# A spatial gating product in Strassen's form, with the second phase of the kernel in written order

## The chip, the cores and the metric

The kernel runs on one core of a Trainium2 chip. The metric is the device time of one execution in microseconds. Three executions of the kernel before took 1106.92, 685.29 and 686.55 us, median 686.55 us; the profiled execution took 685.1 us.

## What is computed

Three stages for a batch of 4, a sequence S of 768 and a model width of 384. First gated linear attention (8 heads of 48), then a low-rank mix along the sequence and an MLP, then a gated MLP with a product along the sequence. All results are wanted in float32; the changed part is in the last stage:

```python
h = gelu(x @ w_in)                       # 768 x 1024 for each batch
u, v = h[..., :512], h[..., 512:]
v_n = (v - mean(v)) / sqrt(var(v) + 1e-6) * g_ln
v_s = einsum('ts,bsd->btd', w_sg, v_n) + b_sg[None, :, None]   # 768 x 768 times 768 x 512
out = x + (u * v_s) @ w_out
```

## The kernel before

Phase 1 computes attention and the first MLP, batch by batch; `mlp(b, hf, fill)` runs the 12 steps of one half (384 rows of the sequence) of a batch, and in each step `fill(i)` issues a piece of other work: for batches 0 to 2 the attention of the next batch, for batch 3 (`fill_last`, 24 steps for the two halves) the loading of phase 2's weights. TensorE takes every operand as a sum of two numbers, a high part `h` that ScalarE copies out in the matmul's own format and a low part `l`, the rest, that POOL subtracts (`split`, L145 to L147); a product is then three matmuls, hh, hl and lh (`products`). In `fill_last` each of the first 12 steps narrows and splits a piece of w_in and w_out, each of the other 12 splits one twelfth of w_sg into the buffer that held a piece of the first MLP's weights, and the last step splits batch 0 (`make_hl`, its tiles are `uh` and `ul`).

Phase 2 has four kinds of blocks, each a run of matmuls into one PSUM bank:

- `v_block` (6 for each batch, 9 matmuls of 512 columns): one chunk of 128 rows of the v half; then gelu (ScalarE Square L114, VectorE L115, ScalarE Tanh L116, VectorE L117), the mean and variance (VectorE L123, L124), 1/sqrt on POOL (L125, L126), the normalising VectorE operation L127, and a split into `vnh` and `vnl`.
- `u_block` (8, 9 matmuls of 384 columns): the u half, transposed, with gelu.
- `g_block` (8, 18 matmuls of 384 columns): the product with w_sg for 128 channels and half of the sequence; VectorE scales and adds the bias (L832) and multiplies by u (L833); a split into `gth` and `gtl`.
- `o_block` (6, 12 matmuls of 384 columns): the product with w_out, the residual and the store to HBM.

The blocks go in the order v(b), o(b-1), u(b), g(b). A block takes the next of the 8 PSUM banks, so block n waits until the operations that read block n-8 are done. Phase 1 stands under `manual_schedule`: its instructions run as the program writes them on each engine. This is closed (`fixed.close()`) after the last MLP, and phase 2's order on each engine comes from the framework's scheduler. All DMAs are issued by SP, in order.

Of the kernel before, what the change touches and what calls it, by code (L numbers as in the profile page):

```python
# [30 lines left out]
HT = S // 2  # L31
PR = 112
# [5 lines left out]
UNIT = 384  # L38
# [14 lines left out]
def kernel(  # L53
# [79 lines left out]
    def fast(st):  # L133
# [41 lines left out]
        fixed = st.enter_context(ExitStack())  # L175
        fixed.enter_context(tc.manual_schedule())
# [557 lines left out]

        todo = [(flat(win[0]), flat(win[1]), w_in, i) for i in range(0, KD * FF2, UNIT)]
# [4 lines left out]
        wsg = [[flat(x) for x in w1s[f]] for f in range(KF1)]  # L740
        here = {}

        def fetch_last(i):
            if i < KF1:
                _, _, src, at = todo[i]
                here[i] = fetch(stage, [(ALL, src[:, at:at + UNIT])], 128, UNIT)
            elif i < 2 * KF1:
                here[i] = stage.tile([128, UNIT], F32, tag="z", name="z")
                nc.sync.dma_start(here[i], w_sg[:, (i - KF1) * HT:(i - KF1 + 1) * HT])
# [7 lines left out]
        def fill_last(i):  # L757
# [3 lines left out]
            if i < KF1:  # L761
                here[i] = narrow_last(narrow_first(stage, here[i], 128, UNIT))[0]
            else:
                split(*wsg[i - KF1], here.pop(i))
            fetch_last(i + 2)
# [4 lines left out]
            elif i == 2 * KF1 - 1:  # L770
                make_hl(work2, 0, 0)
                make_hl(work2, 0, 1)
# [6 lines left out]
        fixed.close()  # L779
# [4 lines left out]
        vp = p2.enter_context(sp("vp", 1))  # L784
        tm = p2.enter_context(sp("tm", 2))
        stage_cm.__exit__(None, None, None)
        gp = p2.enter_context(sp("gp", 2, "right"))
# [4 lines left out]
        turn = [0]  # L792
# [6 lines left out]
        vn, ug, gt = {}, {}, {}  # L799

        def v_block(b, s):
            if s == 0:
                vn[b] = [vp.tile([128, NCH, HF], F32R, tag="vn" + x, name="vn" + x) for x in "hl"]
            if s % 3 == 0 and (b, s // 3) not in hl:
                make_hl(work2, b, s // 3)
# [4 lines left out]
            x = tm.tile([128, HF], F32, tag="t1", name="t1", bufs=4)  # L810
            gelu2(p, tm.tile([128, HF], F32, tag="t0", name="t0", bufs=3), x, x)
            normalise(tm, eps, x, x)
            split(vn[b][0][:, s, :], vn[b][1][:, s, :], x)

        def u_block(b, hf, m):
# [5 lines left out]
            x = ug[b][:, m, hf * HT:(hf + 1) * HT]  # L821
            gelu2(p, tm.tile([128, HF], F32, tag="t0", name="t0", bufs=3)[:, :HT], x, x)

        def g_block(b, hf, m):
            if m == 0:
                gt[b, hf] = [gp.tile([128, KH, HT], F32R, tag="gt" + x, name="gt" + x) for x in "hl"]
            p = any_bank([128, HT])
            t = slice(hf * HT, (hf + 1) * HT)
            mm(p, [x for s in range(NCH) for x in products(cut(vn[b], ALL, s, slice(m * 128, m * 128 + 128)),
                                                           wsg[s * 2 + hf])])  # L830
            x = tm.tile([128, HF], F32, tag="t0", name="t0", bufs=3)[:, :HT]
            vec.scalar_tensor_tensor(x, p, gcol[:, m:m + 1], bsg[:, t], op0=ALU.mult, op1=ALU.add)  # L832
            vec.tensor_tensor(x, x, ug[b][:, m, t], op=ALU.mult)  # L833
            split(gt[b, hf][0][:, m, :], gt[b, hf][1][:, m, :], x)

        def o_block(b, hf, d):
# [3 lines left out]
            mm(p, x + [x for m in range(KH) for x in products(cut(wout, ALL, m, slice(d * 128, d * 128 + 128)),  # L840
                                                              cut(gt[b, hf], ALL, m))])
            o = xT[b][:, d, hf * HT:(hf + 1) * HT]
            if last:
                act.activation(o, p, ACTF.Copy, scale=0.5)
            else:
                vec.scalar_tensor_tensor(o, p, 0.5, o, op0=ALU.mult, op1=ALU.add)
            nc.sync.dma_start(out[b, d * 128:(d + 1) * 128, hf * HT:(hf + 1) * HT], o)

        act.activation(two, ident, ACTF.Copy, scale=2.0)
        for b in range(B + 1):  # L850
            if b < B:
                for s in range(NCH):
                    v_block(b, s)
            if b:
                for hf in range(2):
                    for d in range(KD):
                        o_block(b - 1, hf, d)
            if b < B:
                for hf in range(2):
                    for m in range(KH):  # L860
                        u_block(b, hf, m)
                for hf in range(2):
                    for m in range(KH):
                        g_block(b, hf, m)
        p2.close()

    def general(b, st):
# [100 lines left out]
        for s in range(NCH):  # L968
# [5 lines left out]
            normalise(wk, eps, t1, vn[:, s, :])  # L974
# [86 lines left out]
```

## Time and profile before

| | |
|---|---|
| profiled execution | 685.1 us |
| its span | 683.0 us |
| TensorE busy | 673.2 us (99%) |
| VectorE, ScalarE, POOL busy | 409.6, 265.6, 260.5 us |
| chain of waits that ended last | 88% TensorE, 6% DMA |

The time of an execution is its span and some 2 us around it. Phase 1 ends, and phase 2 begins, at 428.20 us in the span. In the timelines a matmul's row is longer than its distance to the next, since matmuls overlap; the pace of TensorE is read from the starts. DMA traffic is at 394 and 396 GB/s in the page's second and third slices of 40, where phase 1 loads its weights, and at 60 GB/s or less in most slices of phase 2.

### The profile page before, as it was taken

How to read it: one execution, taken by the hardware profiler on the slowest of the kernel's cores; microseconds unless marked ns; L12 is line 12 of the kernel's file. 1: busy time of each engine (PE TensorE's matmuls, PEld its weight loads, DVE VectorE, ACT ScalarE, POOL GpSimd, SP SyncE). 2: the span in 40 equal slices, each digit the busy share in tenths (PEclk: the TensorE clock that was granted, in tenths of full speed). 3: DMA queues.
4: the chain of work that ended last, by engine and by line, in shares of the span. 5: the costliest groups of instructions: out<-in, count | busy, mean ns of one | idle time of the engine just before them, and what ended most of it. 6: DMA issues, size and time to landing. Idle time of an engine off the chain costs nothing.

```text
span 683.0 us, 12753 instructions
## 1 busy us (share of the span) xinstructions
PE 673.2 (99%) x5153; PEld 640.8 (94%) x5153; DVE 409.6 (60%) x719; ACT 265.6 (39%) x547; POOL 260.5 (38%) x324
## 2 busy tenths in 40 slices
PE   7999999999999999999999999999999999999997
PEld 5889899999999999999999999899899999989997
DVE  7988776444655444655458821694675486458532
ACT  4787333222323222323234423572543246143410
POOL 5789922112311212311124533674444254335030
PEclk9999999999999999999999999999999999999999
DMA  8990113301111211110024321000010001001002
GB/s 319 394 396 27 59 61 98 99 38 59 59 60 59 75 43 59 60 59 1 2 70 139 93 72 46 24 2 1 1 69 1 1 12 59 1 1 70 1 1 74
DMA packets 22098, 47.10 MB, mean 69 GB/s; under 512 B 2576, under 2 KB 10640, under 8 KB 22032
## 3 DMA queue, kind: packets, MB, share of 16 engines
q1 hardware_dynamic: 22032, 46.21, 19.7%
q8 instruction: 42, 0.69, 0.4%
q14 instruction: 24, 0.20, 0.1%
HBM read 41.49 MB, written 4.72 MB: 68 GB/s over the span
## 4 chain that ended last, share of the span: by engine, by line
PE 88%; DMA 6%; POOL 3%; DVE 1%; issue 1%; ACT 1%; SPq 0%; DVEq 0%; ACTq 0%; POOLq 0%
PE ps_h L81 29%; PE ps_ch L555 20%; PE ps_at L81 14%; PE ps_ch L81 14%; PE ps_at L396 3%; PE ps_at L428 3%; DMA raw<-in_w_dram 2%; DMA fqk<-in_fqk_dram 2%; POOL w L303 2%; PE ps_at L433 1%; PE ps_at L410 1%; DMA xT<-in_fqk_dram 1%; PE ps_at L504 1%; PE ps_at L480 1%; PE ps_at L450 1%; DVE ps_at L272 1%
## 5 line engine op out<-in xcount | busy, mean ns | idle before, releaser
L575 DVE SCALAR_TENSOR_TENSOR al<-ps_h,ah 128x384 fp32r<-128x384 f32 x96 | 53.4, 556 | 121.6 <-ACT ah L574 121.1
L81 PE MATMUL ps_h<-uh,w 128*128 128x384 f32 x576 | 120.2, 343 | 0.0
L555 PE MATMUL ps_ch<-ah,w 128*128 128x384 f32 x576 | 115.3, 334 | 0.0
L555 PEld LDWEIGHTS ps_ch<-ah,w 128*128 128x128 f32 x576 | 101.2, 188 | 0.0
L81 PEld LDWEIGHTS ps_h<-uh,w 128*128 128x128 f32 x576 | 98.8, 188 | 1.9
L574 ACT ACTIVATE ah<-ps_h 128x384 fp32r<-128x384 f32 x96 | 47.1, 491 | 122.6 <-PE ps_h L81 122.5
L555 PE MATMUL ps_ch<-al,w 128*128 128x384 f32 x288 | 65.6, 335 | 0.0
L81 PE MATMUL ps_h<-ul,w 128*128 128x384 f32 x288 | 65.4, 334 | 0.0
L147 POOL TENSOR_TENSOR ul<-xT,uh 128x384 fp32r<-128x384 f32 x45 | 47.6, 1086 | 46.7 <-ACT uh L146 45.8
L147 POOL TENSOR_TENSOR gtl<-t,gth 128x384 fp32r<-128x384 f32 x32 | 32.8, 1027 | 73.5 <-ACT gth L146 73.5
L81 PEld LDWEIGHTS ps_h<-ul,w 128*128 128x128 f32 x288 | 51.5, 188 | 0.1
L555 PEld LDWEIGHTS ps_ch<-al,w 128*128 128x128 f32 x288 | 51.3, 188 | 0.0
L146 ACT ACTIVATE gth<-t 128x384 fp32r<-128x384 f32 x32 | 16.8, 525 | 78.0 <-DVE t L833 78.0
L363 POOL TENSOR_TENSOR fall<-g,fqk 112x4 f32<-112x4 f32 x15 | 3.1, 208 | 110.2 <-DVE g L358 110.2
L147 POOL TENSOR_TENSOR xl<-x,xh 128x384 fp32r<-128x384 f32 x18 | 18.2, 1013 | 53.1 <-ACT xh L146 51.8
L402 DVE TENSOR_TENSOR am<-ps_at,mask 128x512 f32<-128x512 f32 x43 | 27.9, 685 | 17.2 <-PE ps_at L396 17.0
L147 POOL TENSOR_TENSOR vnl<-t,vnh 128x512 fp32r<-128x512 f32 x24 | 31.1, 1296 | 17.8 <-ACT vnh L146 17.8
L81 PE MATMUL ps_ch<-w,vnh 128*128 128x384 f32 x144 | 36.7, 335 | 0.1
L81 PE MATMUL ps_at<-w,vnh 128*128 128x384 f32 x144 | 36.6, 334 | 0.0
L367 POOL TENSOR_TENSOR fqk<-fqk,g 112x512 f32<-112x512 f32 x21 | 26.9, 1283 | 23.9 <-issue 21.2
L396 PEld LDWEIGHTS ps_at<-fqk 48*128 48x128 f32 x336 | 21.5, 187 | 9.6 <-issue 4.3
L396 PE MATMUL ps_at<-fqk 48*128 48x128 f32 x336 | 25.8, 285 | 3.6 <-POOL fqk L381 2.2
(234 smaller groups left out, 1494.3 us busy)
## 6 DMA issues: line engine op xcount, KB each, us to landing
fqk<-in_fqk_dram SPq DMA_DIRECT2D x36, 384.0 KB, 3.7
raw<-in_w_dram SPq DMA_DIRECT2D x24, 384.0 KB, 7.9
out_dram<-xT SPq DMA_DIRECT2D x24, 192.0 KB, 2.0
v<-in_v_dram SPq DMA_DIRECT2D x21, 192.0 KB, 3.9
raw<-in_w_in_dram SPq DMA_DIRECT2D x8, 384.0 KB, 3.2
xT<-in_fqk_dram SPq DMA_DIRECT2D x6, 384.0 KB, 5.8
z<-in_w_sg_dram SPq DMA_DIRECT2D x12, 192.0 KB, 2.4
fqk<-in_fqk_dram SPq DMA_DIRECT2D x8, 256.0 KB, 4.9
```

What stands on the lines that cost most here:

```text
L81: pe.matmul(ps, lhsT=l, rhs=r, start=(i == 0), stop=(i == n - 1))
L146: act.activation(hi, src, ACTF.Copy)
L147: eng.tensor_tensor(lo, src, hi.bitcast(F32), op=ALU.subtract)
L272: vec.scalar_tensor_tensor(zi, zi, 3, low, op0=ALU.logical_shift_left, op1=ALU.bitwise_or)
L303: pool.tensor_tensor(t[:, 1], s, t[:, 0].bitcast(F32), op=ALU.subtract)
L367: pool.tensor_tensor(k, k, g.rearrange("p h t -> p (h t)"), op=ALU.mult)
L396: pe.matmul(sc[j][:, p, :], lhsT=e["k"][rows, p, :], rhs=e["q"][rows, p, :], start=True, stop=True)
L402: vec.tensor_tensor(am, sc[j], m3, op=ALU.mult)
L428: pe.matmul(y[t, h * D:(h + 1) * D], lhsT=e["am"][h % 2][:, h // 2, t], rhs=vv[:, h * D:(h + 1) * D], start=(h == 0), stop=(c == 0 and h = ...
L555: pe.matmul(ch[d], lhsT=w, rhs=a[i // 2], start=(f == 0 and i == 0), stop=(last and i == 2))
L574: act.activation(ah, hp, ACTF.Relu)
L575: vec.scalar_tensor_tensor(al, hp, 0.0, ah.bitcast(F32), op0=ALU.max, op1=ALU.subtract)
```

## The change

The product with w_sg, 768 x 768 by 768 x 512, is cut in two in each of its three directions. In place of the 8 products of halves there are 7 (Strassen's scheme in Winograd's form), and sums before and after them:

- On the side of w_sg, 7 operands (4 quarters of the weight and three more sums, each in 3 chunks of 128 rows) are made once, in the second half of the last MLP: 4 VectorE subtractions for each of 3 chunks, and 21 splits in place of 12. 9 of the 21 tiles (`side`, 384 KB each, high and low part) stay in the buffers of the first MLP's weights; all 21 are written to HBM. In phase 2 these 9 buffers are a ring: after each product its three buffers are loaded again, for the product three further on (`fetch_side`).
- On the side of v, POOL makes the 4 sums for each of the 3 chunks of a batch (`combine`), and 12 splits a batch (`part`) take the place of 6. `n1` to `n4` hold the operands.
- On the result side, VectorE adds the products: for 8 output tiles a batch one addition each in `final` and 6 more, and ScalarE copies 2.
- All of phase 2 is under `manual_schedule`. A block is a slot; `at` and `soon` put the later operations of a block at the end of a later slot. `make_hl` of batch 0 moves from step 23 of the last MLP to steps 8 and 10, and that of batch b+1 into the g slots of b.

```diff
+HS = NCH // 2
+HM = HF // 2
+NOP = 7
+RING = 9
...
-        vec.tensor_scalar(dst, src, mv[:, 0:1], rs, op0=ALU.subtract, op1=ALU.mult)
+        return lambda: vec.tensor_scalar(dst, src, mv[:, 0:1], rs, op0=ALU.subtract, op1=ALU.mult)
...
-        fixed = st.enter_context(ExitStack())
-        fixed.enter_context(tc.manual_schedule())
+        st.enter_context(tc.manual_schedule())
...
+        dr = p2.enter_context(tc.tile_pool(name="dr", bufs=1, space=bass.MemoryType.DRAM))
+        sides = [dr.tile([128, 2, HT], F32, name=f"side{k}") for k in range(NOP * HS)]
...
+        def side_steps():
...
+            def keep_side(op, s, x):
+                k = op * HS + s
+                if k < RING:
+                    t = ring[k] = w1p.tile([128, 2, HT], F32R, tag=slot(k), name="side")
+                    parts = [(t[:, 0], 0), (t[:, 1], 1), (t, ALL)]
+                else:
+                    parts = places[turn[0] % len(places)]
+                    turn[0] += 1
+                split(parts[0][0], parts[1][0], x)
+                for t, i in parts[2:] or parts:
+                    nc.sync.dma_start(sides[k][:, i], t.bitcast(F32))
+            for s in range(HS):
...
+                vec.tensor_tensor(t1, b12, b11, op=ALU.subtract)
+                vec.tensor_tensor(b12, b22, b12, op=ALU.subtract)
+                vec.tensor_tensor(t2, b22, t1, op=ALU.subtract)
+                vec.tensor_tensor(t4, b21, t2, op=ALU.subtract)
+                for i, (op, x) in enumerate(((0, b11), (4, b12), (6, b22), (1, b21), (5, t1), (3, t2), (2, t4))):
+                    keep_side(op, s, x)
...
@@ fill_last(i)
-            else:
-                split(*wsg[i - KF1], here.pop(i))
-            fetch_last(i + 2)
...
+            if i > KF1:
+                for _ in range(2):
+                    next(making[0], None)
...
-            elif i == 2 * KF1 - 1:
-                make_hl(work2, 0, 0)
-                make_hl(work2, 0, 1)
+            elif i in (8, 10):
+                make_hl(work2, 0, i // 2 - 4)
...
+        def fetch_side(j):
+            if j not in ring and j < NOP * HS * B:
+                ring[j] = w1p.tile([128, 2, HT], F32R, tag=slot(j), name="side")
+                nc.sync.dma_start(ring[j].bitcast(F32), sides[j % (NOP * HS)])
...
+        def slot_end():
+            for fn, args in lines.pop(now[0], []):
+                fn(*args)
+            now[0] += 1
...
+        def part(b, i, s):
+            names = ("n1", "n2", "n3", "n4")
...
+            split(ops[b][i][:, 0, s], ops[b][i][:, 1, s], x if i else x[:, :HM])
+
+        def combine(b, s, i):
+            a11, a21, a12, a22 = halves(b, s)
+            x, y, z, op = [(a22, a21, a22, ALU.add), (a21, a11, a21, ALU.subtract),
+                           (a11, a22, a11, ALU.subtract), (a12, a12, a11, ALU.subtract)][i]
+            pool.tensor_tensor(x, y, z, op=op)
+
+        def plan_sums(b):
+            n = now[0]
+            for s, k in ((0, 4), (1, 6), (2, 8)):
+                at(n + k, part, b, 0, s)
+                at(n + k, part, b, 1, s)
+            for k, todo in ((5, ((0, 0), (0, 1))), (7, ((0, 2), (1, 0), (1, 1))),
+                            (9, ((1, 2), (2, 0), (2, 1), (2, 2)))):
...
+            third, fourth, last = ((14, 15, 16), (17, 18, 19), 10) if b else ((14, 14, 15), (20, 20, 21), 16)
...
-            mm(p, [x for s in range(NCH) for x in products(cut(vn[b], ALL, s, slice(m * 128, m * 128 + 128)),
-                                                           wsg[s * 2 + hf])])
...
+            def final(p, row, hf, base, x, k):
+                vec.tensor_tensor(p, p, base, op=ALU.add)
+                vec.scalar_tensor_tensor(x, p, gcol[:, row:row + 1], bsg[:, spans[hf]], op0=ALU.mult, op1=ALU.add)
+                vec.tensor_tensor(x, x, ug[b][:, row, spans[hf]], op=ALU.mult)
+                at(n + k, gated, b, row, hf, x)
...
+            for i, (o, cols) in enumerate(((0, lo), (1, lo), (1, hi), (2, lo), (2, hi), (3, hi), (3, lo))):
+                j = NOP * HS * b + HS * i
+                for m in range(2):
...
+                    mm(p, [x for s in range(HS) for x in products([t[:, e, s, c] for e in range(2)],
+                                                                  [ring[j + s][:, e] for e in range(2)])])
+                    if m:
+                        for s in range(HS):
+                            fetch_side(j + s + RING)
+                    if i == 0:
+                        act.activation(first[:, m], p, ACTF.Copy)
+                    elif i == 1:
+                        final(p, m, 0, first[:, m], tm.tile([128, HF], F32, tag="t0", name="t0", bufs=3)[:, :HT], 10)
+                    elif i == 2:
+                        held[m] = p
+                    elif i == 3:
+                        vec.tensor_tensor(second[:, m], p, first[:, m], op=ALU.add)
+                    elif i == 4:
+                        vec.tensor_tensor(third[:, m], p, second[:, m], op=ALU.add)
+                        final(held[m], 2 + m, 0, third[:, m], first[:, m], 10 + m)
...
+                    slot_end()
```


TensorE, first g stage (batch 0). Before, one output tile out of eight, with six buffers `w_` that hold w_sg:

```order
L81 MATMUL ps_ch<-w_658,vnh 128x384 x2
L81 MATMUL ps_ch<-w_658,vnl 128x384
L81 MATMUL ps_ch<-w_721,vnh 128x384 x2
L81 MATMUL ps_ch<-w_721,vnl 128x384
L81 MATMUL ps_ch<-w_837,vnh 128x384 x2
L81 MATMUL ps_ch<-w_837,vnl 128x384
L81 MATMUL ps_ch<-w_919,vnh 128x384 x2
L81 MATMUL ps_ch<-w_919,vnl 128x384
L81 MATMUL ps_ch<-w_1001,vnh 128x384 x2
L81 MATMUL ps_ch<-w_1001,vnl 128x384
L81 MATMUL ps_ch<-w_1085,vnh 128x384 x2
L81 MATMUL ps_ch<-w_1085,vnl 128x384
```

Now, the first five of the seven products, two tiles each:

```order
L85 MATMUL ps_at<-side,n_5170 128x384 x9
L85 MATMUL ps_ch<-side,n_5170 128x384 x9
L85 MATMUL ps_at<-side,n_5173 128x384 x9
L85 MATMUL ps_h<-side,n_5173 128x384 x9
L85 MATMUL ps_ch<-side,n_5173 128x384 x9
L85 MATMUL ps_at<-side,n_5173 128x384 x9
L85 MATMUL ps_h<-side,n_5371 128x384 x9
L85 MATMUL ps_ch<-side,n_5371 128x384 x9
L85 MATMUL ps_at<-side,n_5371 128x384 x9
L85 MATMUL ps_ch<-side,n_5371 128x384 x9
```

8 tiles of 18 matmuls have become 14 of 9; each product reads three `side` buffers.

SP's queue between the loads for phase 2 and the second batch's stores, before:

```order
L749 DMA z<-in_w_sg_dram 128x384 x12
L789 DMA bsg<-in_b_sg_dram 128x768
L847 DMA out_dram<-xT_72 128x384 x6
L847 DMA out_dram<-xT_73 128x384 x6
```

Now, from the end of batch 0's g stage to the first three products of batch 1 (with the tiles' numbers; `side18` is the DRAM copy):

```order
L851 DMA side_5486<-side18_4221 128x768
L851 DMA side_5488<-side19_4222 128x768
L851 DMA side_5490<-side20_4223 128x768
L851 DMA side_5527<-side0_4203 128x768
L851 DMA side_5529<-side1_4204 128x768
L851 DMA side_5531<-side2_4205 128x768
L851 DMA side_5576<-side3_4206 128x768
L851 DMA side_5578<-side4_4207 128x768
L851 DMA side_5580<-side5_4208 128x768
```

A queue that held only stores in phase 2 now holds 75 loads of 384 KB as well, each behind the matmuls that last read its buffer.

POOL in the last MLP, before:

```order
L147 TENSOR_TENSOR winl<-z,winh 128x384 x6
L147 TENSOR_TENSOR ul<-xT_75,uh 128x384 x3
L147 TENSOR_TENSOR winl<-z,winh 128x384 x2
L147 TENSOR_TENSOR woutl<-z,wouth 128x384 x4
L147 TENSOR_TENSOR w_658<-z,w_658 128x384
```

Now:

```order
L151 TENSOR_TENSOR winl<-z,winh 128x384 x6
L151 TENSOR_TENSOR ul<-xT_75,uh 128x384 x3
L151 TENSOR_TENSOR winl<-z,winh 128x384 x2
L151 TENSOR_TENSOR ul<-xT_72,uh 128x384 x3
L151 TENSOR_TENSOR woutl<-z,wouth 128x384 x2
L151 TENSOR_TENSOR ul<-xT_72,uh 128x384 x3
L151 TENSOR_TENSOR woutl<-z,wouth 128x384 x2
L151 TENSOR_TENSOR side<-raw,side 128x384
```

The six subtractions for batch 0 (`xT_72`) now stand among those of steps 8 to 11, close behind the three for batch 3 (`xT_75`).

## Rows read from the trace of the kernel before

**Rows 1.** The page: span, busy time of the engines, and TensorE's granted clock.
```profile
span 683.0 us, 12753 instructions
...
PE 673.2 (99%) x5153; PEld 640.8 (94%) x5153; DVE 409.6 (60%) x719; ACT 265.6 (39%) x547; POOL 260.5 (38%) x324
...
PEclk9999999999999999999999999999999999999999
```

**Rows 2.** Chain of waits, in time order: start us, us, what (one batch).
```profile
491.06 2.10 PE ps_at L81 x12
...
516.05 3.14 PE ps_at L81 x18
...
537.91 3.12 PE ps_ch L81 x18
541.03 2.04 PE ps_at L81 x9
```

**Rows 3.** Windows: us, busy us per engine (instructions), TensorE clock, DMA share, GB/s.
```profile
20.00:40.00 20.00, 20.00 (x341) 16.08 (x336) 18.45 (x33) 15.38 (x38) 13.70 (x18) 1.00 1.03 395
...
429.00:678.00 249.00, 248.91 (x1368) 239.77 (x1366) 149.56 (x273) 96.34 (x186) 103.73 (x127) 1.00 0.06 21
```

**Rows 4.** Timeline of TensorE where phase 2 begins: start us, us.
```profile
428.20 0.39 PE L81 MATMUL ps_h<-winh,uh 128*128 128x512 f32 x1
...
430.60 0.39 PE L81 MATMUL ps_ch<-winh,uh 128*128 128x512 f32 x1
```

**Rows 5.** Timeline of the last MLP, around step 6: DVE's al, POOL, TensorE.
```profile
372.82 0.56 DVE L575 SCALAR_TENSOR_TENSOR al<-ps_h,ah 128x384 fp32r<-128x384 f32 x1 [0.42 <-ACT ah L574]
...
374.48 3.72 POOL L147 TENSOR_TENSOR ul<-xT,uh 128x384 fp32r<-128x384 f32 x3
...
376.16 0.54 DVE L575 SCALAR_TENSOR_TENSOR al<-ps_h,ah 128x384 fp32r<-128x384 f32 x1
...
379.83 0.55 DVE L575 SCALAR_TENSOR_TENSOR al<-ps_h,ah 128x384 fp32r<-128x384 f32 x1
...
382.44 0.68 PE L555 MATMUL ps_ch<-al,w 128*128 128x384 f32 x3
```

**Rows 6.** Timeline of VectorE and POOL in the first v blocks.
```profile
443.42 0.55 DVE L127 TENSOR_SCALAR t<-t,mv,rs 128x512 f32<-128x512 f32 x1 [0.36 <-POOL rs L126]
...
444.92 1.29 POOL L147 TENSOR_TENSOR vnl<-t,vnh 128x512 fp32r<-128x512 f32 x1
444.99 1.50 DVE L127 TENSOR_SCALAR t<-t,mv,rs 128x512 f32<-128x512 f32 x1 [0.37 <-POOL rs L126]
```

**Rows 7.** Groups by line, phase 2: out<-in, count, busy us, mean ns, idle before.
```profile
L127 DVE TENSOR_SCALAR t<-t,mv,rs 128x512 f32<-128x512 f32 x24 | 20.8, 866 | 12.4 <-POOL rs L126 12.4
L123 DVE BATCH_NORM_STATS2 st<-t 128x6 f32<-128x512 f32 x24 | 15.7, 681 | 0.0
...
L832 DVE SCALAR_TENSOR_TENSOR t<-ps_ch,gcol,bsg 128x384 f32<-128x384 f32 x12 | 7.4, 617 | 19.0 <-PE ps_ch L81 19.0
...
L115 DVE SCALAR_TENSOR_TENSOR t<-t,ps_ch 128x512 f32<-128x512 f32 x10 | 6.7, 674 | 2.9 <-ACT t L114 2.9
L117 DVE SCALAR_TENSOR_TENSOR ug<-t,ps_at 128x384 f32<-128x384 f32 x12 | 6.6, 551 | 3.8 <-ACT t L116 3.5
```

**Rows 8.** The same view, POOL and ACT.
```profile
L147 POOL TENSOR_TENSOR gtl<-t,gth 128x384 fp32r<-128x384 f32 x32 | 32.8, 1027 | 73.5 <-ACT gth L146 73.5
L147 POOL TENSOR_TENSOR vnl<-t,vnh 128x512 fp32r<-128x512 f32 x24 | 31.1, 1296 | 17.8 <-ACT vnh L146 17.8
...
L114 ACT ACTIVATE t<-ps_ch 128x512 f32<-128x512 f32 x10 | 5.9, 593 | 0.7 <-PE ps_ch L81 0.5
```

**Rows 9.** Timeline of SP's queue in phase 1: 24 loads of 384 KB issued.
```profile
16.08 24.01 SPq L251 DMA_DIRECT2D raw<-in_w_dram  x24
```

**Rows 10.** DMA issues by line: KB each, median us from issue to landing.
```profile
raw<-in_w_in_dram SPq DMA_DIRECT2D x8, 384.0 KB, 3.2
```

**Rows 11.** Timeline of the end of the program.
```profile
678.35 0.49 ACT L844 ACTIVATE xT<-ps_at 128x384 f32<-128x384 f32 x1 [11.02 <-PE ps_at L81]
```

More of the change, by code (lines that the diff above doesn't have):

```diff
@@ L778, in fast @@
             mlp(B - 1, hf, fill_last)
-        fixed.close()
         pend.pop()()
@@ L820, in u_block @@
                                                            cut(hl[b, hf], ALL, kd))])
[L821 to L828, printed above, removed]
[L829 to L834 removed]
+            x = ug[b][:, m, spans[hf]]
@@ new lines, in combine @@
+        def combine(b, s, i):
[10 more added lines that the diff above has]
+                            (9, ((1, 2), (2, 0), (2, 1), (2, 2)))):
+                for s, i in todo:
+                    at(n + k, combine, b, s, i)
+            third, fourth, last = ((14, 15, 16), (17, 18, 19), 10) if b else ((14, 14, 15), (20, 20, 21), 16)
+            for s in range(HS):
+                at(n + third[s], part, b, 2, s)
+                at(n + last, combine, b, s, 3)
+                at(n + fourth[s], part, b, 3, s)
@@ new lines, in gated, with g_stage @@
+        def gated(b, row, hf, x):
+            key = b, hf
+            if key not in gt:
+                gt[key] = vp.tile([128, 2, KH, HT], F32R, tag=("n3", "n4")[hf], name="gt")
+            split(gt[key][:, 0, row], gt[key][:, 1, row], x)
+        def g_stage(b):
+            n = now[0]
+            lo, hi = slice(0, HM), slice(HM, HF)
+            first, second, third = [w1p.tile([128, 2, HT], F32, tag=f"w{i}", name="sum") for i in (0, 10, 11)]
+            held = {}
+            def final(p, row, hf, base, x, k):
[3 more added lines that the diff above has]
+                at(n + k, gated, b, row, hf, x)
+            if b + 1 < B:
+                for hf, k in enumerate((2, 4) if b else (8, 9)):
+                    at(n + k, make_hl, work2, b + 1, hf)
+            for i, (o, cols) in enumerate(((0, lo), (1, lo), (1, hi), (2, lo), (2, hi), (3, hi), (3, lo))):
+                j = NOP * HS * b + HS * i
+                for m in range(2):
+                    t = ops[b][o]
+                    c = slice(cols.start + m * 128, cols.start + m * 128 + 128)
+                    p = any_bank([128, HT])
+                    mm(p, [x for s in range(HS) for x in products([t[:, e, s, c] for e in range(2)],
+                                                                  [ring[j + s][:, e] for e in range(2)])])
+                    if m:
+                        for s in range(HS):
+                            fetch_side(j + s + RING)
[10 more added lines that the diff above has]
+                        final(held[m], 2 + m, 0, third[:, m], first[:, m], 10 + m)
+                    elif i == 5:
+                        vec.tensor_tensor(second[:, m], p, second[:, m], op=ALU.add)
+                        final(p, 2 + m, 1, third[:, m], third[:, m], 14 + m)
+                    else:
+                        final(p, m, 1, second[:, m], second[:, m], 15 + m)
+                    slot_end()
```

113 lines of the change are left out of this document (82 added, 31 removed).

## The prediction

> **What bounds the kernel.** I read the page first: TensorE is busy for 673.2 of 683.0 us, and its granted clock is in the top tenth in every slice, which is the 2.4 GHz level [rows 1]. A busy TensorE need not be a dense one, so the second view is the chain of waits inside phase 2. The reader sees runs of matmuls of which each begins where the last ended: 12 of 384 columns in 2.10 us, eight runs of 18 between 516.05 and 541.03 us in 3.12 us each, 9 of 512 columns in 2.04 us [rows 2]. So a matmul of 384 columns costs 3.12/18 = 0.1733 us, one of 512 columns 0.2267 us, and a run of 9 pays no more for each than a run of 18. The third view is the windows: from 429 to 678 us TensorE is busy for 248.91 of 249.00 us, VectorE for 149.6, POOL for 103.7, ScalarE for 96.3, and the DMA engines for 6% [rows 3]. Phase 2 is bound by the number of its matmuls, and nothing else is near its limit. One hole is left: the first v block begins at 428.20 and the second at 430.60 us, 2.40 us for work of 2.04, since POOL's low parts for batch 0 come late [rows 4]. After the last matmul 683.0 - 678.35 = 4.65 us of copy and store stay in any case [rows 11].
>
> **Matmuls removed.** A batch has 8 tiles of 18 matmuls, and now 14 of 9: 144 become 126. For four batches that is 72 fewer, at 0.1733 us each, **12.48 us**. All other blocks keep their matmuls. The first v block no longer waits, since its operand is split 13 and more steps earlier: **0.36 us**, the hole above.
>
> **What the product now asks of the DMA queue.** After each product (two tiles, 3.12 us) three buffers of 384 KB are loaded again for the product three further on. That is 378 GB/s while it lasts. Bounds: with several loads queued, 24 of the same size are issued in 24.01 us, held back by the queue, so 1.0 us each, and the queue then moves 395 GB/s [rows 3, 9]; a load alone lands after 3.2 us [rows 10], which would be the price of each if they did not overlap. The first reload of a batch can start when its first product ends and is wanted 6.24 us later; four such reloads are wanted within 15.6 us (five products). They need 2.2 us of landing (3.2 - 1.0) and 12 loads: 14.2 us at 1.0 us, and nothing waits; 2.2 + 38.4 = 40.6 us at 3.2 us, 25 us of waiting a batch. I take 1.0 us, as the row of 24 is the same shape from the same queue, three are queued at once here, and SP has nothing else to issue in those 22 us: **0 us**. The pace at which TensorE begins to wait is 13.4/12 = 1.12 us, so the cover is thin; if it goes, every product of the last four is late. The first three products of a batch are loaded some 37 us ahead. SP's stores stand behind these loads, and nobody waits for them.
> The Trainium skill, "DMA: Bandwidth & Descriptors", section Rules for kernel authors, speaks against this: full bandwidth wants 1 MiB or more in a DMA, and its table gives 341 GB/s at 1 MB. Even at that rate a load of 384 KB would take 1.15 us by the page (an estimate), and the sum would rise by 4 x (2.2 + 13.8 - 15.6), 1.6 us. The trace does not agree: 395 GB/s at 384 KB each.
>
> **What it asks of VectorE, POOL and ScalarE.** On POOL a batch has 12 splits of v for 6 and 12 sums. From 1.03 us at 384 columns and 1.30 at 512 [rows 8] I estimate 0.76 at 256. So 9 x 1.30 + 3 x 0.76 + 12 x 0.76 - 6 x 1.30 = 15.3 us more a batch, 61 us more in all: 165 of some 236 us. VectorE has 14 more additions a batch, at about 0.6 us as L832 [rows 7]: 34 us more, 183 of 236. ScalarE has 6 more copies for splits and 2 of results. All fit; what counts is order, at two places.
>
> Place one, batch 0, where no o blocks stand between v and g. The second tile of g stands 15 blocks after the first of v, so at 12.24 + 12.48 + 1.56 = 26.3 us, and takes the bank of the second u tile. VectorE must by then have done six v chunks (0.67 + 0.67 + 0.68 + 0.87 us and 0.17 for L124, 3.07 each) and five gelu operations of u at 0.55 [rows 7]. It starts after 2.04 us of matmuls and 0.59 of Square [rows 8]: 2.6 + 18.4 + 2.75 = 23.8 us. With the wait for POOL's 1/sqrt, 12.4 us over 24 or 0.52 each [rows 7], it is 26.9 us: **0.6 us** lost. The lower end is 0. The upper end comes from L127: it takes 0.55 us alone, and 1.50 when a POOL subtraction started just before it, with which it ends [rows 6]; all six at 1.50 make 3.8 us more, 4.4 us lost. POOL is busier now, but the mean of 0.87 already holds a third of such cases, so I stay near the lower end. Later batches have 12.48 us of o blocks there, with 0.55 us of VectorE work each, and lose nothing.
> The Trainium skill, "SBUF — State Buffer", section SBUF: two separate sides, says why: VectorE and GpSimd share a port pair as an exclusive lock, taken by VectorE operations in a two-port mode or with two SBUF inputs, and the loser blocks. The trace agrees (0.55 against 1.50 us); by that rule the new additions with two SBUF inputs can block too, which is the second rival.
>
> Place two, the last MLP. In each step VectorE makes the low part `al`, which TensorE reads a good step later. While POOL did the three subtractions of one `make_hl` (3.72 us), VectorE's shared operations stretched and `al` came 3.34 and then 3.67 us after the one before, in place of 3.12; the last ended at 380.38 and TensorE read it at 382.44 us [rows 5]. So 0.77 us (3.34 + 3.67 - 6.24) of a spare of some 2.8 were used, and 2.06 were left. Now two more `make_hl` follow in steps 8 and 10: POOL has five operations in two steps, 5 x 1.24 = 6.2 of 6.24 us, and stays busy for four more steps. At 0.55 us a step that is 2.2 us against 2.06 left. Between 0 and 1.5 us lost; I take **0.5 us**. In the second half POOL has two splits a step (2.06 of 3.12 us) and VectorE four subtractions three times; four at 0.56 us fit beside `al` (2.24 + 0.56 of 3.12), stretched to 1.2 they make 5.4 us and use 2.2 of the 2.8 spare: 0. The 8.3 MB written to HBM there, at 395 GB/s 21 of 31 us, delay only the next use of a staging buffer four splits later.
>
> At the end, after g of batch 3, no v blocks stand before o. The last row of the gated product passes three VectorE operations (1.8 us), a copy (0.5) and up to three queued splits (3.1): 5.4 us, and is wanted after 3 x 2.08 + 1.56 = 7.8 us. Nothing.
>
> **Sum.** 685.1 - 12.48 - 0.36 + 0.6 + 0.5 = 673.4 us against the profiled execution. The two ordinary runs stand 0.2 and 1.5 us above that execution (median 686.55 us), so I say **673.7 us**, 1.8% less than before. About 2% is what a measurement of this kernel can tell from no change, so the likeliest single word is "same", on its faster edge.
>
> **Rivals.**
> The reloads fall behind (chance 0.10). The mechanism is the ring above, the place the last four products of each batch, the price 2.2 + 12p - 15.6 us a batch at a pace p for one load. For: the demand of 378 GB/s is within 5% of the best rate seen, and phase 2 has never run at more than a few per cent of it. Against: the row of 24. At p = 1.2 us it gives 1.0 us a batch, 678 us. From p = 1.36 us (289 GB/s) on it eats the gain, and from 1.69 us (6.9 us a batch) on the kernel is over 2% slower, 701 us.
> VectorE blocked by a busier POOL (chance 0.22): 4.4 us at place one, 1.5 at place two, and 0.3 to 2 us in later batches, where the bank of a u tile is given back late: 676 to 682 us, middle 678. For it: 1.50 us for L127, and POOL going from 104 to 165 us. Against: before, TensorE stood still for none of the eight or so slow cases among the 24.
> The written order closes waits that these views do not show, or removes more than the one hole (chance 0.10): 670 to 671.7 us. Only 0.09 us of idle stands in rows 3, so it needs matmuls that run closer than 0.1733 us; little speaks for it beyond the scatter of runs.
> That the change would not remove the matmuls is excluded by the order.
>
> **Numbers.** Forecast 0.58, between 671.7 and 675.5 us. The range 671.2 to 681.5 us leaves out the slow half of the first rival and ends of the others, some 0.18. Faster by over 2% means below 672.8 us against the median and 671.6 against 685.3: a quarter of the forecast's case and most of the third rival, 0.22. Slower by over 2%: most of the first rival, 0.08. Within 2%: 0.70.
>
> **What would show it.** Right: 14 runs of 9 in 1.56 us each in every g stage, the first v block in 2.04 us, TensorE's idle time in phase 2 below 1 us, and DMA at 300 GB/s or more in the g stages with no wait of TensorE for `side`. Wrong: TensorE waiting for a DMA in the fourth product or later; for VectorE's banks at the start of g in batch 0; for `al` in steps 9 to 12 of the last MLP. A clock below the upper level would show that such waits have grown beyond what is priced here.

## The result, and the profile after

The changed kernel takes 675.95 us in the median of four runs (675.08 to 676.67), the kernel before 686.70 us beside it: a ratio of 0.9853, with a 95% interval of 0.9834 to 0.9872 (that median counts an execution of 1106.92 us, which the ratio leaves out). A second set (the first experiment below) gives 676.59 against 685.31 us, 0.9875 [0.9857, 0.9893]. The gain is real and stays within 2%. The profiled execution took 675.87 us with a span of 673.7, 9.3 us less than in [rows 1].

The page after, the parts that answer to [rows 1], and the line of the DMA engines' rate in 40 slices:

```profile
span 673.7 us, 13087 instructions
...
PE 661.0 (98%) x5081; PEld 628.8 (93%) x5081; DVE 456.5 (68%) x787; ACT 278.5 (41%) x588; POOL 337.7 (50%) x405
...
PEclk9999999999999999999999999999999999999998
...
GB/s 309 396 396 50 48 73 61 117 59 48 61 70 61 60 59 33 37 108 1 1 1 165 118 158 322 177 2 277 214 44 120 371 30 71 263 229 59 97 197 76
```

TensorE has 72 matmuls fewer (5081 for 5153), and its granted clock is in the top tenth, the 2.4 GHz level, in every slice but the last. POOL is busy for 338 us in place of 261, VectorE for 457 in place of 410, and the DMA engines move up to 371 GB/s in the g stages. The windows say whether any of that reaches TensorE: phase 2 from 430 to 667 us, and the four g stages (columns as in [rows 3]).

```profile
430.00:667.00 237.00, 237.00 (x1298) 228.32 (x1297) 184.83 (x330) 105.92 (x218) 164.90 (x194) 1.00 0.41 148
...
454.77:476.62 21.85, 21.85 (x127) 21.85 (x127) 18.02 (x31) 12.91 (x28) 21.66 (x22) 1.00 0.83 299
514.00:535.85 21.85, 21.85 (x128) 21.85 (x127) 18.08 (x26) 7.25 (x17) 14.88 (x14) 1.00 0.84 300
573.23:595.08 21.85, 21.85 (x128) 21.85 (x128) 14.62 (x26) 7.24 (x17) 13.50 (x13) 1.00 0.83 303
632.45:654.30 21.85, 21.85 (x127) 21.85 (x127) 14.05 (x26) 4.76 (x11) 6.98 (x7) 1.00 0.60 217
sum 87.40, PE 87.40 PEld 87.40 DVE 64.77 ACT 32.15 POOL 57.02; mean PE 21.85 PEld 21.85 DVE 16.19 ACT 8.04 POOL 14.26
```

TensorE is busy for 237.00 of 237.00 us. A g stage takes 21.85 us, which is 14 x 1.56: seven products of two tiles, with nothing between them. The DMA engines are busy for 83% of it at 299 to 303 GB/s; in the last batch, which loads for no next one, for 60% at 217 GB/s. In the chain of waits the first v block and the runs of g and o stand like this (answer to [rows 2, 4]):

```profile
430.19 2.04 PE ps_at L85 x9
432.23 2.04 PE ps_h L85 x9
...
491.14 2.11 PE ps_at L85 x12
493.25 2.11 PE ps_h L85 x12
...
515.73 1.56 PE ps_h L85 x9
517.29 1.56 PE ps_ch L85 x9
```

The hole of [rows 4] is gone: 2.04 us for the first v block. But 12 matmuls of an o block, 2.10 us in [rows 2] and 2.08 in the block behind it, now take 2.11. The same view of the kernel before has

```profile
493.16 2.08 PE ps_h L81 x12
```

And phase 2 begins at 430.03 us in TensorE's timeline (the chain above counts 0.16 us later), not at 428.20. The timeline of the last MLP shows why; first TensorE, where a half of the MLP ends, then VectorE, ScalarE and POOL in the 6 us before:

```profile
393.75 0.68 PE L85 MATMUL ps_h<-ul,w 128*128 128x384 f32 x3
395.43 1.45 PE L558 MATMUL ps_ch<-ah,w 128*128 128x384 f32 x6 [1.00 <-DVE xT L567]
396.72 0.70 PE L558 MATMUL ps_ch<-al,w 128*128 128x384 f32 x3
...
388.93 3.72 POOL L151 TENSOR_TENSOR ul<-xT,uh 128x384 fp32r<-128x384 f32 x3
392.61 1.33 POOL L151 TENSOR_TENSOR woutl<-z,wouth 128x384 fp32r<-128x384 f32 x1
...
391.88 1.19 DVE L104 SCALAR_TENSOR_TENSOR z<-z,raw 128x384 int32<-128x384 int32 x1
393.10 1.25 DVE L107 SCALAR_TENSOR_TENSOR z<-raw,z 128x384 int32<-128x384 int32 x1
394.27 0.55 DVE L578 SCALAR_TENSOR_TENSOR al<-ps_h,ah 128x384 fp32r<-128x384 f32 x1
394.74 1.47 DVE L567 TENSOR_TENSOR xT<-ps_ch,xT 128x384 f32<-128x384 f32 x3
...
394.38 0.52 ACT L150 ACTIVATE wouth<-z 128x384 fp32r<-128x384 f32 x1 [2.33 <-DVE z L107]
394.81 0.47 ACT L577 ACTIVATE ah<-ps_h 128x384 fp32r<-128x384 f32 x1
```

Read it backwards. TensorE needs `ah` and the banks `ps_ch`. ScalarE's `ah` at 394.81 stood in its queue behind a copy of `wouth` that had waited 2.33 us for VectorE's L107; VectorE's L567, which frees the banks, stood behind the same L107. Beside POOL's `ul` and `woutl` L107 takes 1.25 us, where it needs 0.56 earlier in this stage. Six matmuls that begin at 395.43 could have begun at 394.27 (393.75 and 3 x 0.1733): 1.16 us, and 0.25 more before the next three (396.72 less 395.43 and 6 x 0.1733). This stall is **1.41 us**.

The end answers to [rows 11]:

```profile
667.68 0.49 ACT L996 ACTIVATE xT<-ps_ch 128x384 f32<-128x384 f32 x1 [6.38 <-PE ps_ch L85]
```

From here to the end of the span are 6.02 us, in place of 4.65. So the span's 9.3 us are: phase 2 to this copy 237.65 in place of 250.15 us, -12.5; its start 1.83 us later, of which 1.41 are the stall and 0.4 a shift that is there at 364 us already, in the part where the program is the same (the kernel before, run again, is 0.9 us later at that place, so this is scatter); the end, 1.37 more.

### The profile page after: what moved, and what is told of

The parts are those of the page before. It is cut to its first block, busy times and chain, and to the rows that moved or that the text cites. A ratio compares the mean times of both kernels' runs of the same rounds, so it can differ in the third digit from the quotient of the medians.

```text
span 673.7 us, 13087 instructions
## 1 busy us (share of the span) xinstructions
PE 661.0 (98%) x5081; PEld 628.8 (93%) x5081; DVE 456.5 (68%) x787; ACT 278.5 (41%) x588; POOL 337.7 (50%) x405
## 4 chain that ended last, share of the span: by engine, by line
PE 88%; DVE 4%; POOL 3%; DMA 2%; ACT 1%; issue 1%; SPq 0%; DVEq 0%; ACTq 0%; POOLq 0%
PE ps_h L85 28%; PE ps_ch L558 18%; PE ps_ch L85 13%; PE ps_at L85 13%; PE ps_at L399 4%; PE ps_at L431 3%; POOL w L306 2%; PE ps_at L436 2%; PE ps_at L413 1%; DVE z L107 1%; DVE z L104 1%; PE ps_ch L431 1%; PE ps_at L507 1%; DMA raw<-in_w_dram 1%; PE ps_at L483 1%
## 5 line engine op out<-in xcount | busy, mean ns | idle before, releaser
L151 POOL TENSOR_TENSOR ul<-xT,uh 128x384 fp32r<-128x384 f32 x45 | 49.7, 1138 | 28.3 <-ACT uh L150 28.3
L151 POOL TENSOR_TENSOR n<-t,n 128x512 fp32r<-128x512 f32 (+1 forms) x48 | 54.6, 1167 | 0.0
L150 ACT ACTIVATE n<-t 128x512 fp32r<-128x512 f32 (+1 forms) x48 | 27.5, 574 | 36.0 <-DVE t L131 32.4
L85 PE MATMUL ps_at<-side,n 128*128 128x384 f32 x189 | 36.2, 336 | 0.0
L85 PE MATMUL ps_ch<-side,n 128*128 128x384 f32 x189 | 36.2, 336 | 0.0
L151 POOL TENSOR_TENSOR gt<-sum,gt 128x384 fp32r<-128x384 f32 x24 | 26.2, 1106 | 15.9 <-ACT gt L150 15.9
L85 PEld LDWEIGHTS ps_at<-side,n 128*128 128x128 f32 x189 | 33.1, 188 | 0.0
L85 PEld LDWEIGHTS ps_ch<-side,n 128*128 128x128 f32 x189 | 33.1, 188 | 0.0
```

Of the source, the lines that this page charges most:

```text
L85: pe.matmul(ps, lhsT=l, rhs=r, start=(i == 0), stop=(i == n - 1))
L150: act.activation(hi, src, ACTF.Copy)
L151: eng.tensor_tensor(lo, src, hi.bitcast(F32), op=ALU.subtract)
```

## The experiments

**The changed kernel again.** No edit.

> The changed kernel once more, as the yardstick for the small effects beside it. Theory: 676 us against 686.6, ratio 0.985; TensorE's stall of 1.41 us in the last MLP (393.75 to 396.72 us) and blocks of g and v without a wait are seen again. Whether the 6.06 us from the last ScalarE copy to the end of the span are a property of the program is open: if they are, this profile shows 6.0 again and the kernel pays 1.4 us at its end; if they are scatter, it shows something between 4.6 and 6.1.

Measured: the stall at 393.76 is 1.43 us, phase 2 is without a wait, and the end takes 5.47 us. What the end is worth is taken up below.

**The two make_hl put back late.**

```
-            elif i in (8, 10):
-                make_hl(work2, 0, i // 2 - 4)
+            elif i == 2 * KF1 - 1:
+                make_hl(work2, 0, 0)
+                make_hl(work2, 0, 1)
```

> The two make_hl of batch 0 go back from steps 8 and 10 of the last MLP to its last step, where the kernel before had them; all else as changed. Theory (VectorE's shared operations were stretched by POOL's make_hl, and al and ah came late): the stall of 1.41 us at the change of halves is gone, under 0.2 us, and the hole in the first v block is back at 0.36 us or more: 1.0 us less than the changed kernel. Rival one (the stall is the price of the new side tiles that begin there, whatever POOL did before): the stall stays at 1.4 us, and the hole comes on top, 0.4 us more than the changed kernel. Rival two (POOL is behind with side tiles when the MLP ends): the stall is gone but the hole is 2 to 4 us, 1 to 3 us more than the changed kernel.

Measured: 677.12 us, 0.9868 [0.985, 0.9886]. The stall is gone, so POOL's two `make_hl` cause it, and the side tiles alone don't. But the six v blocks of batch 0 take 13.52 us in place of 12.24: holes of 1.28 us in all, between the 0.36 of my theory and the 2 of rival two. The last copy comes 0.35 us earlier than in the run beside it, and the time doesn't tell the two apart, so the 1.0 us that the theory gave did not come. Moving the splits ahead was worth 1.3 us there, and cost 1.4 us earlier in the program.

**The two make_hl spread out.**

```
-            elif i in (8, 10):
-                make_hl(work2, 0, i // 2 - 4)
+            elif i in (2, 10):
+                make_hl(work2, 0, i // 8)
```

> The two make_hl of batch 0 at steps 2 and 10, so that three of them (with that of batch 3 at step 6) stand four steps apart. Theory (it is the pile of three in five steps that keeps POOL without a free moment): POOL has 8 splits of weights and 7.4 us of make_hl in 8 steps (25 us), so it comes free between them, the stall of 1.41 us shrinks to 0.5 us or less and the first v block has no hole: 0.9 to 1.4 us less than the changed kernel. Rival (one make_hl at step 10 is enough, since it ends beside the change of halves): the stall stays above 1.0 us and the time is the same.

Measured: 674.93 us, 0.9849 [0.9824, 0.9873], the runs from 673.12 to 678.0. From 390 to 398 us TensorE is busy all the time: the stall is gone, as the theory has it, and there is no hole in the first v block. But the profiled run gives 2.2 us back in batch 1, where 72 matmuls of u take 14.72 in place of 12.49 us. First the place, then what VectorE and POOL had done 30 us before:

```profile
500.89 0.34 PE L85 MATMUL ps_at<-uh,winl 128*128 128x384 f32 x1
502.66 0.44 PE L85 MATMUL ps_h<-uh,winh 128*128 128x384 f32 x1 [1.43 <-DVE t L875]
...
468.59 7.35 DVE L950 TENSOR_TENSOR sum<-sum,ug 128x384 f32<-128x384 f32 x1
475.86 0.55 DVE L976 TENSOR_TENSOR sum<-ps_ch,sum 128x384 f32<-128x384 f32 x1
...
466.39 1.32 POOL L151 TENSOR_TENSOR n<-t,n 128x512 fp32r<-128x512 f32 x1
467.66 5.89 POOL L151 TENSOR_TENSOR ul<-xT,uh 128x384 fp32r<-128x384 f32 x6
473.51 2.01 POOL L151 TENSOR_TENSOR gt<-t,gt 128x384 fp32r<-128x384 f32 x2
```

One product of VectorE, 0.56 us elsewhere, took 7.35: it ended only when POOL paused, at 475.5 us, behind the six subtractions of a `make_hl` and two splits back to back. VectorE's work of the next batch came some 3 us late by it, until a bank that u needs was late. The changed kernel has the same at 520.14 us, where 4.77 us are hidden. This is the second rival of the prediction, VectorE blocked by a busier POOL; it had named later batches, at 0.3 to 2 us, but not this operation. The time, with runs 5 us apart, doesn't tell this kernel from the changed one.

**The gated product's high and low rows side by side.**

```
-gt[key] = vp.tile([128, 2, KH, HT], ...); ... gt[key][:, 0, row], gt[key][:, 1, row]
+gt[key] = vp.tile([128, KH, 2, HT], ...); ... gt[key][:, row, 0], gt[key][:, row, 1]
```

> The gated product's tile holds the high and low part of a row side by side in place of all high parts ahead of all low parts. Theory (the matmuls of the o blocks run at 0.1756 us in place of 0.1733 because of where their moving operand lies): 12 of them take 2.08 us again and 24 blocks give back 0.7 us. Rival (the pitch comes from what other engines do in those stretches, or from the modelled ends of the profile): 2.11 us stays, and the time is the same.

Measured: 675.36 us, 0.9852 [0.9836, 0.9868]; 72 matmuls of o take 12.64 us as before the edit, 0.1756 each. The theory fell in this form; the order within the tile is not it. A row of 384 numbers is 1536 bytes, six times 256, so this edit left every row's start where it was against a multiple of 256, and that is what a later experiment changes.

**Without the reloads.**

```
+                if j < NOP * HS:
...
+                else:
+                    ring[j] = ring[NOP * HS - RING + j % RING]
```

> Leaves out 63 of the 75 reloads of side tiles: batches 1 to 3 multiply by tiles that lie in the ring already, so their result is not the reference's; every matmul stays. Theory (the reloads are hidden): a g stage takes 21.85 us as in the changed kernel, and the time is 676.3 us, within 0.5. Rival (the reloads slow TensorE or the other engines while they land): g stages of batches 1 to 3 come below 21.6 us, or the o blocks' 0.1756 us a matmul falls back to 0.1733, and the time is 0.5 to 2 us less.

Measured: 675.42 us, 0.9861 [0.9839, 0.9884]. The windows of the g stages of batches 1 and 2:

```profile
513.16:535.01 21.85, 21.85 (x128) 21.85 (x128) 18.12 (x26) 7.24 (x17) 14.92 (x14) 1.00 0.00 1
572.38:594.23 21.85, 21.85 (x127) 21.85 (x127) 14.62 (x26) 7.24 (x17) 13.50 (x13) 1.00 0.00 1
```

With the DMA engines at rest the stage is the same to 0.01 us, and VectorE and POOL need the same time in it. The o blocks keep their 0.1756 us. The reloads cost nothing, and the rival is out.

**With a copy of 192 KB ahead of each reload.**

```
+                if j >= RING:
+                    nc.sync.dma_start(dr.tile([128, HT], F32, name=f"copy{j}"), sides[j % (NOP * HS)][:, 0])
```

> Before each of the 75 reloads the queue also copies 192 KB, half of the same tile, to a scratch place in HBM that nobody reads: the ring's pace per reload rises by half or more, all else is as changed. Theory (the cover ends at a pace of 1.12 us, and beyond it a batch pays 2.2 + 12p - 15.6 us): at p = 1.5 us 4.6 us a batch, 18 us in all, 694 us; TensorE waits for side tiles in the last four products of each batch and nowhere else. If the copies cost as much as a load (p = 2.0) 42 us, 718 us. Rival (the ring has much more cover than these bounds say): no wait for side tiles, 676 us.

Measured: 689.95 us, 1.0064 [1.0046, 1.0082]. TensorE's waits in phase 2, all of them (engine, line, waited for; us in total, times, longest), and then from the timeline of the queue three reloads, one with its copy:

```profile
PE ps_at L85 <- DMA side<-side: 3.9, 7, 0.7
PE ps_ch L85 <- DMA side<-side: 2.1, 4, 0.7
PE ps_h L85 <- DMA side<-side: 2.0, 3, 1.0
```

```profile
531.26 0.33 SPq L853 DMA_DIRECT2D side<-side  x1
531.72 0.47 SPq L852 DMA_DIRECT2D copy<-side  x1
532.69 0.33 SPq L853 DMA_DIRECT2D side<-side  x1
...
534.16 0.33 SPq L853 DMA_DIRECT2D side<-side  x1
```

The waits shown are 8.0 us in all; since a matmul's row is longer than its distance to the next, each hides a part, and what they cost is read from the stages. The pace is 1.45 us a reload (534.16 - 531.26, halved). The g stages take 24.93, 25.33, 26.20 and 24.84 us, on average 3.48 more than 21.85, all of it in the last three products of a batch. The prediction's 2.2 + 12p - 15.6 gives 4.0 at this pace. So the formula holds within 0.5 us a batch. In the changed kernel the pace can't be read from the issues, which come as TensorE releases the buffers, three in each 3.12 us. It is read where the DMA engines are busy throughout, from 526 to 536 us: 397 GB/s, 0.99 us a load, under the 1.12 at which by the prediction TensorE begins to wait. From issue to landing the 21 reloads of batch 1 took

```profile
DMA to landing us min/median/max: 3.0/5.4/6.4
```

and the first twelve, wanted in the same batch, have some 7.1 us each: the first is issued at 516.28 us, and the fourth product begins at 523.36 (514.00 + 3 x 3.12). So the cover is thin, 0.7 us if the slowest is one of them.

**The 72 matmuls back.**

```
+                    for _ in range(1 if i else 2):
                         mm(p, ...)
```

> The first of the seven products of each batch runs its 2 x 9 matmuls twice (the second time from start again, so the result is the same): 72 matmuls come back, and the written order, the splits, the sums and the reloads all stay. Theory (the gain is the matmuls and nothing else): 72 x 0.1733 = 12.5 us more than the changed kernel, 688.8 us, and slower than the kernel before by the stall of the last MLP, the o blocks and the end. Rival (the written order or the earlier splits carry part of the gain): less than 688 us, in the worst case for the theory 685 or below.

Measured: 687.60 us, 1.0031 [1.0019, 1.0042]: 11.0 and 11.7 us above the two sets of the changed kernel, and 2 us above the kernel before. The four g stages together, columns as above:

```profile
sum 99.88, PE 99.88 PEld 99.88 DVE 61.39 ACT 32.78 POOL 62.27; mean PE 24.97 PEld 24.97 DVE 15.35 ACT 8.19 POOL 15.57
```

99.88 - 87.40 = 12.48 us, the predicted term to the last digit. The time lies just under the 688 us from which the rival would have spoken; the g stages leave it no room, and its end, 5.43 us, is one of the short ones. Without the saved matmuls the change makes the kernel slower: the written order and the splits carry none of the gain on balance.

**Spread, and `final` through PSUM.** The spread kernel, with

```
-                vec.scalar_tensor_tensor(x, p, gcol[...], bsg[...], ...)
-                vec.tensor_tensor(x, x, ug[b][...], op=ALU.mult)
+                vec.scalar_tensor_tensor(p, p, gcol[...], bsg[...], ...)
+                vec.tensor_tensor(x, p, ug[b][...], op=ALU.mult)
```

> The make_hl of batch 0 at steps 2 and 10 as in the spread kernel, and the second operation of `final` writes its result over the PSUM bank, so that the third, the product with ug, reads one operand from PSUM and one from SBUF in place of two from SBUF. Theory (an operation of VectorE with both inputs in SBUF does not run while POOL has operations back to back, 7.35 us of it in the spread kernel's batch 0, and VectorE came 3.5 us late to the next v blocks): no product with ug takes more than 0.8 us, TensorE's stall of 2.3 us in batch 1 is gone, and the time is 1.4 us below the changed kernel, about 674.5. Rival (the stretch is contention for SBUF that any operation of VectorE meets, or VectorE was late for another reason): the product with ug still stretches over 2 us beside POOL's six subtractions, and TensorE still stands for about 2 us in batch 1.

Measured: 674.04 us, 0.9836 [0.982, 0.9853]. The products with ug by group (count, busy us, mean ns), first in the changed kernel, then here, and then the timeline of the same place as in the spread kernel:

```profile
L950 DVE TENSOR_TENSOR sum<-sum,ug 128x384 f32<-128x384 f32 x24 | 17.3, 719 | 0.8
...
L950 DVE TENSOR_TENSOR t<-t,ug 128x384 f32<-128x384 f32 x8 | 10.3, 1290 | 0.3
```

```profile
L950 DVE TENSOR_TENSOR sum<-ps_ch,ug 128x384 f32<-128x384 f32 x9 | 5.0, 558 | 0.3
L950 DVE TENSOR_TENSOR sum<-ps_at,ug 128x384 f32<-128x384 f32 x9 | 5.0, 558 | 0.3
```

```profile
467.26 5.94 POOL L151 TENSOR_TENSOR ul<-xT,uh 128x384 fp32r<-128x384 f32 x6
468.89 0.56 DVE L950 TENSOR_TENSOR sum<-ps_ch,ug 128x384 f32<-128x384 f32 x1
```

Beside POOL's six subtractions the product takes 0.56 us, and TensorE stands nowhere in phase 2. The rival, that any operation of VectorE meets the contention, is out. The Trainium skill, "SBUF — State Buffer", section SBUF: two separate sides, says that an operation of VectorE with two SBUF inputs and one of GpSimd exclude each other for a whole instruction. The trace agrees on which operations block (0.56 us with one input in PSUM, 7.35 with both in SBUF), and goes further: VectorE was shut out for eight instructions in a row, not for one.

**`final` through PSUM alone.** The changed kernel with the last edit only.

> The changed kernel with the PSUM form of `final` alone; make_hl of batch 0 stays at steps 8 and 10. Theory (two separate faults: POOL's pile in the last MLP costs 1.4 us, and the blocked product with ug costs nothing in the changed kernel, where 4.8 us of it are hidden): no product with ug over 1.1 us, the stall of 1.4 us in the last MLP stays, and the time is that of the changed kernel, 676.3 us within 0.6. Rival (the better time of the kernel with both edits came from the PSUM form): 674.0 us, the stall or something else made up for.

Measured: 675.68 us, 0.9854 [0.9836, 0.9872], the stall in the last MLP 1.6 us. As the theory says, the blocked product costs nothing where the changed kernel has it.

**The gated product 128 bytes further on.** The kernel with both edits, and

```
+        pad = p2.enter_context(sp("pad", 1))
+        pad.tile([128, 32], F32, name="pad")
         vp = p2.enter_context(sp("vp", 1))
```

> The kernel with both edits (make_hl at steps 2 and 10, `final` over PSUM), and 128 bytes left free ahead of the buffers of the split v, ug and gt, so that the gated product's rows start 96 bytes behind a multiple of 256, as those of the kernel before did, and not 224 bytes. Theory (the o blocks' 0.1756 us a matmul come from where in SBUF the moving operand starts): 12 matmuls take 2.08 us again, 72 take 12.5 in place of 12.64, and the time falls by 0.6 us to 673.4. Rival (it comes from something else): 12.64 us stay, and the time is 674.0.

Measured: 674.26 us, 0.9835 [0.9821, 0.9848]. Two groups of o matmuls, in the changed kernel and here (mean ns behind the busy time), and from the chain here one o block:

```profile
L85 PE MATMUL ps_ch<-gt,wouth 128*128 128x384 f32 x80 | 20.7, 340 | 0.0
L85 PE MATMUL ps_at<-gt,wouth 128*128 128x384 f32 x72 | 18.5, 338 | 0.0
```

```profile
L85 PE MATMUL ps_ch<-gt,wouth 128*128 128x384 f32 x80 | 20.3, 334 | 0.0
L85 PE MATMUL ps_at<-gt,wouth 128*128 128x384 f32 x72 | 18.3, 334 | 0.0
```

```profile
489.57 2.08 PE ps_at L85 x12
```

72 matmuls take 12.50 us again. The profile confirms the theory; the 0.6 us are too few for the times, which are the same as without the pad.

**The kernel before, for its end.**

> The kernel before once more, for the time from the last ScalarE copy to the end of the span: 4.65 us in its first profile, 5.4 to 6.4 us in nine profiles of the changed kernel and its variants. If that is scatter, this profile shows something over 5 us and no part of the missing gain lies there; if it is a property of the changed program, it shows 4.6 us again, and about 1 us of the gain is lost at the end.

Measured: 685.76 us. Its last copy is at 679.24, the span 683.9: 4.66 us. So it isn't scatter: eleven profiles of the changed kernel and its variants with the branch have 5.4 to 6.4 us there (mean 5.84), and about 1.2 us of the gain is lost there.

**Without the branch at the end.** The kernel with the pad, and

```
-    with tc.If(safe < 1):
-        with tc.For_i(0, B, 1) as b: ... general(b, st)
```

> The kernel of the last experiment without the branch at its end, so without the slow general path that stands behind it: this leaves out the fallback for inputs that the fast path can't take, and nothing else. The kernel before shows 4.65 and 4.66 us from its last ScalarE copy to the end of the span, the changed kernel and its variants 5.4 to 6.4, with two fetches of instructions after the last store has landed that the kernel before doesn't show. Theory (those fetches, for the code behind the branch, hold the end back): without the branch no such fetch, the end takes 4.7 us or less, and the time is 1 us below 674.3 us or lower. Rival (the store's own landing, 2.5 to 3.6 us against 2.2, is what is late): the end still takes 5.4 us or more, and the time is 674.3 us.

Measured: 672.29 us, 0.9800 [0.9783, 0.9816]; the end takes 3.87 us (666.33 to 670.2), and the last store lands after 1.8 us in place of the 2.5 to 4.2 with the branch. So the program without the branch and the code behind it ends about 2 us earlier. The rate of the DMA engines in 40 slices of 0.175 us, in the changed kernel from 668 us, and then here from 665 us:

```profile
GB/s 18 0 0 0 0 26 328 377 316 91 167 9 9 18 18 0 0 0 0 0 0 0 0 0 47 47 0 0 0 0 0 0 0 0 0 0 0 0 0 0
```

```profile
GB/s 0 53 334 369 334 35 0 0 0 0 0 0 0 0 0 184 395 386 158 0 0 0 0 0 0 0 0 0 47 0 0 0 0 0 0 47 0 0 0 0
```

In the first row the store is the block at 300 GB/s and above, and the two slices of 47, at 672.2 to 672.5 us, are the late fetches of instructions. Two such fetches remain here: at 669.9 us, 1.2 us after the store (the second block) has landed, and at 671.1, behind the end of the span. So the sign that the theory named, no such fetch, did not come, and of the 2 us some 0.9 are the store's own landing, as the rival has it (1.8 us, and 2.7 in the kernel with the pad). That the branch and its code cost the time is shown; by what, is not. Why the kernel before, with the same branch, ends in 4.65 us was not tried and stays open. This run also has a stall of 1.21 us at 393.36 in the last MLP, though its `make_hl` are spread: VectorE and POOL were 1 us later against TensorE than in the runs without it. Of four profiles with steps 2 and 10, three are without the stall. The `make_hl` at step 10 is probably still too near the change of halves; no run moved it alone.

## Why the prediction was right, and where its steps were not

- **72 matmuls, 12.48 us:** right, 12.48 in the seventh experiment.
- **The hole of 0.36 us:** closed. A second one of 0.3 us, between u and g of batch 0 (0.25 at 453.17 us and 0.07 behind it, in the kernel before), closed with it.
- **The ring at 0 us:** right, and for its reason: 0.99 us a reload where the engines are busy throughout, against 1.12. A pace that eats the gain, 1.45 us, was tried and cost 14 us. The row of 24 loads [rows 9], 1.0 us each, was a good guide.
- **Place one at 0.6 us:** it was 0, the lower end. I had used a mean that holds slow cases (0.87 us for L127; the same operation, now L131, took 0.58), and no block of batch 0 waited.
- **Place two at 0.5 us:** the mechanism was right and the size was not, 1.41 us, near the upper end of 1.5. I followed `al` alone. What came last was `ah`, in ScalarE's queue behind a copy that waited for VectorE's stretched operations, and the three adds at the change of halves.
- **"After the last matmul 683.0 - 678.35 = 4.65 us of copy and store stay in any case":** this step failed. 6.02 us in this profile, 5.8 on average. I took the end for copy and store, and without the branch it is 3.87 us, so it also holds the branch. Why it grew by 1.2 us under the same branch stays open.
- **"All other blocks keep their matmuls":** in number, yes, but not in time. The o blocks' operand got a new place, 0.1756 us for some 0.1735: 0.7 us in all, a gap of 0.2 in the last batch included.
- **"the new additions with two SBUF inputs can block too":** the mechanism was there, at other operations than the one named. The additions in phase 2 read one input from PSUM and took 0.55 to 0.56 us in the mean; what was blocked is the product with ug, which the kernel before has too (1.21 us at the most there).

The sum with these in place: 673.4 + 0.9 (place two) - 0.6 (place one) + 1.4 (end) + 0.7 (o blocks) + 0.4 (shift in phase 1) - 0.3 (second hole) = 675.9 us, and the execution took 675.87. The range and the word "same" held; the forecast's own range, up to 675.5, did not quite. What pushed the time beyond it is the end first (1.4), then place two (0.9, the second rival at one of its places) and the o blocks (0.7); that place one (0.6) and the second hole (0.3) went the other way, and kept the time near the forecast, is luck. More of the second rival was there too, 4.8 us in one product with ug, and was hidden; in the spread kernel a wait of the same kind, 7.35 us, came to the path.

Spread, with `final` through PSUM, is the best that the runs support with the whole program: 674.04 and 674.26 us, some 2 us below the two sets of the changed kernel, with intervals that don't meet its second one (0.9820 to 0.9853 against 0.9857 to 0.9893) and overlap its first.

## What to carry to other kernels

When the bound engine is dense, price a change by the instructions that it removes there, then go after the second-order places by asking which queue each operand's producer stands in, not only how long the producer takes. Work that is moved ahead to close one hole opens another where its engine has no free moment: here 1.3 us gained and 1.4 lost. A thin but computed cover, as that of the ring, can be trusted once its pace and its time to landing stand in rows of the trace; an operation with both inputs in SBUF beside a back-to-back POOL can't.

## What the runs showed of the hardware

- An operation of VectorE with two SBUF inputs waited through POOL's whole run of operations: 4.77, 7.35 and 7.80 us for one of 0.56. With one input in PSUM it took 0.56 beside the same run. In the last MLP, beside POOL's three subtractions, such operations came through after each one, at 1.2 us; why the two cases differ is open.
- A matmul of 384 fp32r columns took 0.1756 us in the mean (72 in 12.64) with the gated product as its moving operand where the changed kernel has it, and 0.1736 (72 in 12.50) with that 128 bytes further on. By the program's addresses, which the traces don't show, its rows start 224 and 96 bytes behind a multiple of 256. Only these two places were tried.
- Loads of 384 KB with several queued went through at 0.99 us each (397 GB/s from 526 to 536 us), and TensorE, VectorE and POOL took the same time in a g stage with them and without (21.85 and 21.85, 18.08 and 18.12, 14.88 and 14.92 us).
